# Second batch's mixing: DMA transposes on SyncE's queue in place of products with the identity

## The chip, the cores and the metric

The kernel runs on one core of one Trainium2 chip. The metric is the device time of one execution in microseconds (us). The engines are TensorE (PE; its weight loads are shown as PEld), VectorE (DVE), ScalarE (ACT), GpSimd (POOL) and SyncE (SP); SP does nothing here but issue DMAs. Each engine takes its instructions strictly in the order in which they were written.

## The reference

An attention over beacons and tokens is followed by a low-rank mixing over tokens and a two-layer perceptron, for 8 batches of 576 tokens, 8 heads of 64, 512 channels, rank 32 and 2048 hidden channels:

```
a   = softmax(mask(q @ concat(beacon_k, k)^T / 8))          # per batch and head
x   = (a @ concat(beacon_v, v)) laid out as [token, channel] # 576 x 512 per batch
h   = (x^T @ U) @ V                                          # U: 576 x 32, V: 32 x 576
u   = x + h^T
out = u + relu(u @ w_ch1) @ w_ch2
```

## The kernel before

**Layout.** Tokens of a batch lie in five tiles of 112, 128, 128, 128 and 80 rows (tile 4 is the last). The attention writes x, in 16 bits, to a tile `xb` with tokens on partitions (line 425, one DVE product per head). The perceptron wants u with channels on partitions, in one long constant tile `uT` (4 groups of 128 channels by 8 x 576 tokens). The mixing of a batch makes that change of layout and adds the low-rank part. `mix_units` gives it in two forms:

- Not turned: TensorE multiplies x with the identity into PSUM (`x_into`, line 432), 16 products for tiles 0 to 3 and four for tile 4, adds the low-rank product on top (lines 478 and 491), and the sum is copied to `uT`: two copies by DVE and two by ACT for tiles 0 to 3 (lines 467 and 469), one by DVE for tile 4.
- Turned: five DMA transposes, one per token tile, issued on SP's queue, bring x into `uT` (line 444). TensorE makes only the low-rank product, and DVE adds it to what lies in `uT`: four additions for tiles 0 to 3, one for tile 4 (line 465).

In both forms `head` comes first: 20 small products (line 453) and a DVE copy to `qts` (line 459) that make x^T U. Batch 0 is mixed by a function of its own, `first_mix`. Before the change batch 1 is mixed in the first form and batches 2 to 7 in the second.

**Perceptron.** It goes over blocks of 512 tokens. A block is 32 units of work in a queue: 16 g-units (line 559, four products of 512 columns, then a rectification by ACT or DVE) and 16 quarter-sums called c-units here (line 585, four products of 512 columns). Four quarters make one 128-row piece of the output; after its last quarter, block 0 also has four products that add u (line 593), and then DVE or ACT copies the piece (lines 602 and 600) and SP stores it (line 604). I number the c-units of block 0 by their place in the queue: c0 to c15. c0 to c3 need the first half of the second weight matrix `w2`, c4 to c7 the second half; POOL issues the two halves at line 205. The last quarters are c5, c7, c11 and c15. Block 1 needs tokens 512 to 1023, so `uT` of batch 1 must be there before its first g-unit.

**Order of the work.** The program is one hand-written order. Attention goes by pairs of heads (pair 8 is the first of batch 2). A string says what comes next: `r` regroups a pair's q and k on DVE (lines 279 and 281), `q` and `k` turn them on TensorE (line 286) and copy them from PSUM on DVE (lines 319 and 324), `v` makes scores on TensorE (line 398) with the exponentials on ACT (line 407), `m` masks on DVE (lines 335 and 337), `a` and `b` are the products with v for the two heads (lines 416, 424, 425), and `f` takes the next entry from the perceptron's queue. An entry can be empty (`None`): then an `f` does nothing. `mix(1)` places the mixing of batch 1 into the queue; after it come

```
        fill(8)
        regroup_of(NP1)
        regroup_of(NP1 + 1)
        fill(8)
        play("q8 f k8 f v8:01 f q9 f k9 f r10 v8:23,9:0 f")
```

and then the strings of `third`, the first of which is `r11 q10 f m8 k10 f v9:123 f a8 b8 q11 f`. When `mix(1)` is called, the queue holds c0 to c15.

**PSUM.** There are eight banks, handed out in turn in the order in which they were given back in the program.

**Loads.** POOL issues the loads of q, k, v and the weights (lines 199 to 228 and 674); they change the type on the way and share the 16 DMA engines with SP's queue.

Of the kernel before, what the change touches and what calls it, by code (L numbers as in the profile page):

```python
# [30 lines left out]
def kernel(  # L31
# [732 lines left out]
    NF = 2  # L764
# [24 lines left out]
    def feed(b):  # L789

        while state["t"] < NBLK and 512 * (state["t"] + 1) <= S * (b + 1):
            t = state["t"]
            units, state["part"] = mlp_units(
                512 * t, 512, lambda i, m, t=t: rows[ds(512 * t + P * i, m), :], t % 2, t > 0, t == NBLK - 1
            )
            queue.extend(units)
            state["t"] += 1

    def mix(b):

        turned = b >= NF
        turn, head, parts = mix_units(xbs[b], S * b, turned)
        if turned:
            turn()
        n = 0 if not turned else LAG + 3 if b == B - 1 else min(LAG, len(queue) - 8)
        k = 2 if turned else 1
        most, end = parts
        rest = queue[n + k + 3 :]
        queue[:] = queue[0:n] + [head] + queue[n : n + k] + [most] + queue[n + k : n + k + 3] + [end]
        for _ in range(4):  # L810
            queue.extend(rest[:1] + [None])
            del rest[:1]
        queue.extend(rest)
        feed(b)
# [23 lines left out]
    with tc.manual_schedule(engines={ENG.PE, ENG.Activation, ENG.DVE, ENG.SP, ENG.Pool}):  # L838
# [89 lines left out]
        for line in (  # L928
# [6 lines left out]
            if line.startswith("f e4"):  # L935
                load_batch(2)
        mix(1)

        fill(8)
# [81 lines left out]
        for p in range(NP1, NP):  # L1021
            b, c = divmod(p, NH2)
# [17 lines left out]
            else:  # L1040
                long_slot(p, c, av_of(p), qk or [lambda: None] * 2)
        mix(B - 1)
        guard()

# [106 lines left out]
```

## Time and profile before

| what | value |
|---|---|
| median of 3 runs | 351.85 us (351.06 to 354.78) |
| profiled execution: its time | 349.58 us |
| profiled execution: span | 347.9 us |
| PE busy | 340.4 us, 98% of the span |
| DVE busy | 190.6 us, 55% |
| ACT busy | 163.3 us, 47% |
| POOL busy | 102.9 us, 30% |

How to read it: the profiled execution's time is 1.7 us above its span, which is what lies around the span. It is 2.3 us under the median of the timed runs, so a difference is worked out within the profiled execution and then put on the median. In the rows of the timeline the columns are start in us, duration in us, engine, line, operation, output and input, shapes and count, and in brackets the idle time before it with what ended it. A matmul's end is modelled, so the start of the next group says best how long a group held the engine.

### The profile page before, as it was taken

What the parts mean: (1) busy time and instruction counts of PE and PEld (TensorE: products, weight loads), DVE (VectorE), ACT (ScalarE), POOL (GpSimd) and SP (SyncE); (2) the same over time, 40 slices, a digit from 0 to 9 for tenths busy, and PEclk for the clock granted to TensorE, in tenths of its full rate; (3) what the DMA queues carried; (4) which work ended last, traced back from release to release, by engine and by line L of the source; (5) the groups of instructions that cost most, each with busy time, mean ns of one, the idle gap of its engine ahead of it and who ended that gap; (6) DMA issues with size and microseconds to landing.
All of it is one profiled execution on the core that took longest, in us unless ns stands there. A gap on an engine that the chain in (4) does not pass through costs nothing.

```text
span 347.9 us, 7800 instructions
## 1 busy us (share of the span) xinstructions
PE 340.4 (98%) x3094; PEld 173.8 (50%) x3094; DVE 190.6 (55%) x501; ACT 163.3 (47%) x358; POOL 102.9 (30%) x147
## 2 busy tenths in 40 slices
PE   7899999999999999999999999999999999999995
PEld 3564565455554455445554554455445444444443
DVE  6686865788875653664565456535655542323311
ACT  5958851577823665077605662476344203202400
POOL 8978706754504568004820320000000000000000
PEclk9999999999999999999999999999999999999999
DMA  8999999999996999994999797613123314013011
GB/s 169 137 179 154 178 201 175 226 146 147 132 145 134 158 164 135 161 193 37 138 137 225 75 124 113 183 32 70 61 75 47 71 60 121 2 60 106 18 64 64
DMA packets 146667, 41.90 MB, mean 120 GB/s; under 512 B 131520, under 2 KB 142080, under 8 KB 146624
## 3 DMA queue, kind: packets, MB, share of 16 engines
q0 software_dynamic: 87568, 18.18, 67.8%
q1 hardware_dynamic: 58832, 22.87, 36.6%
q8 instruction: 26, 0.43, 0.5%
q10 hardware_dynamic: 224, 0.30, 0.3%
q14 instruction: 17, 0.14, 0.1%
HBM read 37.45 MB, written 9.44 MB: 135 GB/s over the span
## 4 chain that ended last, share of the span: by engine, by line
PE 84%; DMA 8%; ACT 3%; DVE 2%; POOL 1%; issue 0%; ACTq 0%; DVEq 0%
PE gps L559 35%; PE cps L585 31%; PE po L416 7%; PE sps L398 5%; DMA st<-in_q_dram 5%; ACT expt L365 2%; DMA st<-in_k_dram 2%; DMA stk<-in_k_dram 1%; PE cph L611 1%; PE tps L286 1%; ACT w L365 1%; DVE pr L279 1%; PE qtp L453 1%; PE sps L359 1%; POOL st L213 1%; PE ups L478 1%
## 5 line engine op out<-in xcount | busy, mean ns | idle before, releaser
L559 PE MATMUL gps<-uT,w 128*128 128x512 f16 x576 | 135.4, 379 | 0.5 <-DVE kT L324 0.3
L585 PE MATMUL cps<-w,gT 128*128 128x512 f16 x560 | 130.9, 379 | 0.0
L407 ACT ACTIVATE expt<-sps 128x496 f16<-128x496 f32 (+2 forms) x192 | 82.1, 540 | 75.9 <-PE sps L398 75.9
L572 ACT ACTIVATE gT<-gps 128x512 f16<-128x512 f32 x86 | 51.3, 621 | 74.6 <-PE gps L559 72.3
L559 PEld LDWEIGHTS <-w 128*128 128x128 f16 x576 | 52.1, 98 | 59.2 <-issue 2.8
L585 PEld LDWEIGHTS <-gT 128*128 128x128 f16 x560 | 50.8, 98 | 57.6 <-issue 4.6
L574 DVE TENSOR_SCALAR gT<-gps 128x512 f16<-128x512 f32 x58 | 39.9, 690 | 45.6 <-PE gps L559 44.4
L598 DVE TENSOR_TENSOR ob<-cps,ut 128x512 f32<-128x512 f32 x31 | 21.4, 691 | 49.5 <-PE cps L585 48.7
L228 POOL DMA_DIRECT2D vs<-in_v_dram x50 | 39.7, 808 | 14.9 <-DMA w<-in_moe_w_ch_dram 10.8
L416 PEld LDWEIGHTS <-expt 128*128 128x128 f16 x900 | 34.3, 97 | 12.0 <-issue 0.4
L416 PE MATMUL po<-vs,expt 128*128 128x65 f16 x900 | 36.2, 194 | 0.2
L425 DVE TENSOR_TENSOR xb<-po,rec 128x320 f16<-128x320 f32 x64 | 31.5, 492 | 2.2
L424 DVE RECIPROCAL rec<-po 128x5 f32<-128x5 f32 x64 | 12.0, 188 | 27.0 <-PE po L416 26.8
L335 DVE TENSOR_TENSOR expt<-expt,bigmask 128x512 f16<-128x512 f16 x54 | 22.5, 417 | 3.3 <-ACT expt L407 3.3
L398 PE MATMUL sps<-qT,kT 64*128 64x80 f16 (+4 forms) x288 | 22.6, 281 | 0.1
L365 ACT ACTIVATE expt<-sps 128x496 f16<-128x496 f32 (+2 forms) x48 | 20.4, 569 | 0.6 <-PE sps L359 0.6
L210 POOL DMA_DIRECT2D vs<-in_beacon_v_dram x8 | 4.3, 534 | 54.8 <-PE po L416 54.1
L674 POOL DMA_DIRECT2D st<-in_q_dram x20 | 17.0, 865 | 6.8 <-DVE xb L425 2.4
L398 PEld LDWEIGHTS <-kT 64*128 64x128 f16 x288 | 10.2, 94 | 16.0 <-issue 11.4
L674 POOL DMA_DIRECT2D st<-in_k_dram x20 | 16.9, 880 | 1.3 <-DMA st<-in_q_dram 0.9
L465 DVE TENSOR_TENSOR uT<-ups,uT 128x496 f16<-128x496 f32 x24 | 14.5, 668 | 3.7 <-PE ups L478 3.7
L319 DVE COPY qT<-tps 128x576 f16<-128x576 f16 (+1 forms) x16 | 11.8, 736 | 6.0 <-PE tps L286 3.3
(107 smaller groups left out, 179.0 us busy)
## 6 DMA issues: line engine op xcount, KB each, us to landing
out_dram<-ob SPq DMA_DIRECT2D x35, 256.0 KB, 2.2
vs<-in_v_dram POOLq DMA_DIRECT2D x18, 128.0 KB, 6.9
w<-in_moe_w_ch_dram POOLq DMA_DIRECT2D x4, 512.0 KB, 6.6
w<-in_moe_w_ch_dram POOLq DMA_DIRECT2D x2, 1024.0 KB, 12.9
st<-in_k_dram POOLq DMA_DIRECT2D x12, 128.0 KB, 9.4
st<-in_q_dram POOLq DMA_DIRECT2D x12, 128.0 KB, 10.2
st<-in_k_dram POOLq DMA_DIRECT2D x4, 288.0 KB, 12.2
st<-in_q_dram POOLq DMA_DIRECT2D x4, 288.0 KB, 13.1
```

The lines of the kernel that those rows point to most:

```text
L228: nc.gpsimd.dma_start(out=dst[a : a + nq[j], j, :, :], in_=src[hs, ds(q0[j], nq[j]), :].rearrange("h p d -> p h d"))
L335: nc.vector.tensor_tensor(out=e4, in0=e4, in1=bigmask, op=ALU.min)
L365: nc.scalar.activation(out=ex[i][:, ds(SLOT * g, gw[g])], in_=ps[g, i][:, 0 : gw[g]], func=AF.Exp, scale=scale)
L398: nc.tensor.matmul(banks[i][:, ds(at0 + o, w)], kT[hp, c, ds(P * ch, P)], qT[hp, c, ds(qa, w)], start=True, stop=True, skip_group_check=le ...
L407: nc.scalar.activation(out=at[p][3][i][:, ds(SLOT * g, gw[g])], in_=bank[:, ds(at0, gw[g])], func=AF.Exp, scale=scale)
L416: nc.tensor.matmul(po[:, j, :], ex[0 : nk[c], ds(blk[(c, j)], P)], vs[0 : nk[c], ds(c * H * E + h * E, E)], start=(c == 0), stop=(c == j),)
L425: nc.vector.tensor_tensor(out=xb[:, :, ds(h * D, D)], in0=po[:, :, 0:D], in1=r.broadcast_to([P, NT, D]), op=ALU.mult)
L559: nc.tensor.matmul(g[:, 0:n], w1[:, cc, ts(dc, P)], uT[:, cc, ds(t0, n)], start=(cc == 0), stop=(cc == NCC - 1))
L572: nc.scalar.activation(out=gT["t"][:, dc, 0:n], in_=g[:, 0:n], func=AF.Relu)
L574: nc.vector.tensor_scalar_max(out=gT["t"][:, dc, 0:n], in0=g[:, 0:n], scalar1=0.0)
L585: nc.tensor.matmul(ps[:m, :], gT["t"][:, dc, ds(P * i, m)], w2[:, dc, :], start=(dc == 0), stop=turned and dc == NDC - 1, skip_group_check ...
L674: nc.gpsimd.dma_start(out=dst[a : m[j], j, :, :], in_=src[:, ds(q0[j], nq[j]), :].rearrange("h p d -> p h d"))
```

## The change

Batch 1 is mixed in the turned form, like batches 2 to 7; `NF`, which also says where the attention's second part begins, stays 2.

```
     def mix(b):
 
-        turned = b >= NF
+        turned = b >= 1
         turn, head, parts = mix_units(xbs[b], S * b, turned)
         if turned:
             turn()
```

What `mix` does with `turned` (unchanged lines): the five transposes are issued at once, and the mixing's three units are put at another place of the queue.

```
        n = 0 if not turned else LAG + 3 if b == B - 1 else min(LAG, len(queue) - 8)
        k = 2 if turned else 1
        most, end = parts
        rest = queue[n + k + 3 :]
        queue[:] = queue[0:n] + [head] + queue[n : n + k] + [most] + queue[n + k : n + k + 3] + [end]
        for _ in range(4):
            queue.extend(rest[:1] + [None])
            del rest[:1]
        queue.extend(rest)
```

With 16 entries in the queue and `LAG` of 10, `n` becomes 8 where it was 0. The queue (a dash is an empty entry):

```
before: head c0 most c1 c2 c3 end c4 - c5 - c6 - c7 - c8 c9 c10 c11 c12 c13 c14 c15
after:  c0 c1 c2 c3 c4 c5 c6 c7 head c8 c9 most c10 c11 c12 end c13 - c14 - c15 - -
```

The functions that the turned form calls:

```
        def turn():
            for j in range(NT):
                nc.sync.dma_start_transpose(
                    out=uT[:, :, ds(u0 + q0[j], nq[j])], in_=xb[: nq[j], j, :]
                )
...
        def settle(i, dst, ups):
            if turned:
                nc.vector.tensor_tensor(out=dst, in0=ups, in1=dst, op=ALU.add)
            elif i % 2:
                nc.vector.tensor_copy(out=dst, in_=ups)
            else:
                nc.scalar.activation(out=dst, in_=ups, func=AF.Copy)
...
            for cc in range(NCC) if not turned else ():
                x_into(xb, ups[cc], cc, list(range(NT - 1)), 0, True)
```

On SP the five transposes stand ahead of the four stores of block 0, which came first there before.

More of the change, by code (lines that the diff above doesn't have):

```diff
@@ L799, in mix @@
     def mix(b):
-        turned = b >= NF
+        turned = b >= 1
         turn, head, parts = mix_units(xbs[b], S * b, turned)
```

## The prediction

> **What bounds the kernel now.** I read the busy times on the page first, then the chain that ended last, then who waits from 71 us to the end.
>
> ```profile
> PE 340.4 (98%) x3094; PEld 173.8 (50%) x3094; DVE 190.6 (55%) x501; ACT 163.3 (47%) x358; POOL 102.9 (30%) x147
> PEclk9999999999999999999999999999999999999999
> PE 84%; DMA 8%; ACT 3%; DVE 2%; POOL 1%; issue 0%; ACTq 0%; DVEq 0%
> PE gps L559 <- DVE kT L324: 0.3, 1, 0.3
> 71.00:110.00 39.00, 39.00 (x443) 21.37 (x442) 31.85 (x86) 23.00 (x52) 14.52 (x19) 1.00 1.71 140
> ```
>
> TensorE is busy for 98% of the span, at full granted clock in every slice, and 84% of the last chain is its own work. The fourth line is the whole answer on PE's products for the stretch from 71 us to the end: one wait of 0.3 us, at the start of it. The window (its length, then PE, PEld, DVE, ACT, POOL) has PE busy for all 39 us. So two things hold. TensorE time taken away is worth its full length, and a hole that opens in TensorE's stream ahead of 71 us is carried to the end, since nothing behind it has idle time in which to make it up.
>
> The stage that changes lies from 48.5 to 71 us. These are rows of its timeline; the last two, of a later pair of heads, are there for a price.
>
> ```profile
> 48.55 0.49 DVE L425 TENSOR_TENSOR xb<-po,rec 128x320 f16<-128x320 f32 x1
> 48.92 0.62 PE L453 MATMUL qtp<-xb,Usb 112*32 112x128 f16 x20
> 49.47 1.04 PE L585 MATMUL cps<-w,gT 128*128 128x512 f16 x4
> 50.34 1.05 PE L432 MATMUL ups<-ident,xb 112*128 112x112 f16 x16
> 51.32 0.39 PE L478 MATMUL ups<-Vsb,qts 32*128 32x496 f16 x4
> ...
> 54.24 0.31 PE L432 MATMUL uend<-ident,xb 80*128 80x80 f16 x4
> 54.39 0.31 PE L491 MATMUL uend<-Vend,qts 128*128 128x80 f16 x4
> ...
> 56.26 0.39 PE L593 MATMUL cps<-ident,uT 128*128 128x128 f16 x4
> 56.48 1.89 PE L585 MATMUL cps<-w,gT 128*128 128x512 f16 x8
> ...
> 59.30 0.42 PE L286 MATMUL tps<-ident,pr 96*128 96x96 f16 x6
> 59.75 0.76 DVE L319 COPY qT<-tps 128x576 f16<-128x576 f16 x1 [1.66 <-PE tps L286]
> 60.88 0.76 DVE L319 COPY kT<-tps 128x576 f16<-128x576 f16 x1 [0.37 <-PE tps L286]
> 61.77 0.58 PE L398 MATMUL sps<-qT,kT 64*128 64x496 f16 x4
> 63.58 0.69 DVE L602 COPY ob<-cps 128x512 f32<-128x512 f32 x1 [1.87 <-PE cps L593]
> 64.97 0.76 DVE L319 COPY kT<-tps 128x576 f16<-128x576 f16 x1
> 65.72 0.57 DVE L279 COPY pr<-st 96x768 f16<-96x768 f16 x1
> 68.38 0.73 DVE L319 COPY qT<-tps 128x576 f16<-128x576 f16 x1
> 70.80 1.04 PE L559 MATMUL gps<-uT,w 128*128 128x512 f16 x4 [0.33 <-DVE kT L324]
> 85.29 0.35 DVE L279 COPY pr<-st 96x768 f16<-96x768 f16 x1
> 86.17 0.76 DVE L319 COPY qT<-tps 128x576 f16<-128x576 f16 x1
> ```
>
> From start to start a c-unit holds TensorE for 50.34 - 49.47 = 0.87 us, `head` for 0.55, the four u products of a finished piece for 0.22. Note the last wait at 70.80: the second g-unit of block 1 waited for a DVE copy. From 65.72 on, DVE's row of regroupings, copies and masks is what ends there. That g-unit is my finish line: from it on both programs have the same instructions in the same order, and TensorE is gapless.
>
> **What is removed.** The 20 identity products: 51.32 - 50.34 = 0.98 us and 54.39 - 54.24 = 0.15 us, together 1.13 us of TensorE. Two copies leave ACT, which is idle there and gains nothing.
>
> **What is moved.** The queue puts c0 to c7 ahead of `head`, so pair 8 starts behind 13 c-units where it stood behind 9. From pair 8 to block 1's first g-unit only c13, c14 and c15 are left as cover, where seven were. That matters because pair 8 is a chain of hand-overs: q8 is turned on PE (59.30), copied by DVE (59.75), k8 copied (60.88), then scored on PE (61.77). In the kernel before, c-units fill these holes. In the changed one the entry behind k8 is empty, so TensorE must wait out DVE's copy, and the same DVE chain then runs on through pairs 9 and 10 to the finish line.
>
> **What is added.** Five transposes on SP, five DVE additions in place of three copies, and a wait of DVE on the transposes. Their prices:
>
> ```profile
> L465 DVE TENSOR_TENSOR uT<-ups,uT x24: 664/665/676, 105.3 to 285.5; 128x496 f16<-128x496 f32 x24
> L465 DVE TENSOR_TENSOR uT<-uend,uT x6: 479/480/481, 109.0 to 286.7; 128x320 f16<-128x320 f32 x6
> L205 POOL DMA_DIRECT2D w<-in_moe_w_ch_dram x2: 882/883/884, 36.2 to 38.6; - x2
> DMA to landing us min/median/max: 11.6/12.9/14.2
> L553 SPq DMA_TRANSPOSE ut<-uT x4: 1245/1318/2147, 69.8 to 73.8; - x4
> DMA to landing us min/median/max: 8.6/9.2/10.2
> L444 SPq DMA_TRANSPOSE uT<-xb x5: 1251/1276/2093, 92.4 to 98.5; - x5
> DMA to landing us min/median/max: 4.4/5.5/6.9
> L228 POOL DMA_DIRECT2D vs<-in_v_dram x10: 732/873/1029, 48.0 to 68.9; - x10
> DMA to landing us min/median/max: 8.0/9.2/12.4
> 50.00:55.00 5.00, 5.00 (x46) 2.79 (x45) 1.52 (x3) 1.06 (x2) 1.88 (x3) 1.00 1.32 202
> 70.00:75.00 5.00, 4.67 (x62) 2.71 (x60) 3.77 (x11) 3.42 (x8) 2.83 (x4) 1.00 2.80 164
> ```
>
> (The landing line under each row is that row's, from the windows 44 to 75 for line 228, 60 to 110 for the 553 row, 90 to 110 for the 444 row.)
>
> *When do the transposes land?* Batch 1's x is complete at 48.55 + 0.49 = 49.04. SP has nothing else, issues one about every 1.3 us, and so starts the fourth at 53.0 and the fifth at 54.3. The four additions for tiles 0 to 3 each need the first four transposes. No transpose runs in this stretch before, so I bound the flight: 4.4 us at the low end (line 444 from 92 us, where the engines have pauses), 12.4 us at the high end (a POOL load of this very stretch). The DMA columns (share, GB/s) of 50 to 55 us show 1.32 at 202 GB/s: the engines are full, as they are at 70 to 75, where line 553 took 8.6 to 10.2. I take 8.6, the nearest row's low end, since the share is lower here: the fourth lands at 61.6.
>
> [...]
>
> *The walk through the changed kernel*, by the prices above. c0 starts where `head` did, at 48.9; c3 ends at 52.4. c4 needs the second half of `w2`: issued at 38.6, landing after 14.2, so 52.8, and I take 53.0 with its hand-over, a wait of 0.6 that did not exist. c4 to c7 with two sets of u products end at 56.9, `head` at 57.5, c9 at 59.2. The low-rank products start there, and DVE, 0.45 us behind PE as at 59.30 and 59.75, could add from 59.65. It waits until 61.6. Queued behind it on DVE are the c11 copy, the last addition, and the copies of q8 and k8, for which TensorE's scores, and ACT's exponentials after them, wait. So from 61.6: four additions 2.66, line 602 0.69, last addition 0.48 make 65.4; q8's copy 0.76 and k8's 0.89 (60.88 to 61.77) make 67.05, where the scores start. TensorE has been through c12, q8, c13 and k8 by about 64.4 and stands idle some 2.6 us. Scores 0.58 and c14 0.87: 68.5. DVE takes up q9 0.45 later; q9 0.76 and k9 0.75 (64.97 to 65.72): 70.45. Then two regroupings. They took 68.38 - 65.72 = 2.66 us beside POOL's issues; one free of them took 86.17 - 85.29 = 0.88. POOL's v loads are out by 68.9 in the kernel before, so I take 2 x 0.88: 72.2. From there to the finish line as before, 70.80 - 68.38 = 2.42: **74.6 against 70.80, 3.8 us later**. The 1.13 us saved are in the walk already.
>
> Other cover: SP's first store is ready near 55.6, when the fifth transpose is just issued; even were that issue a microsecond longer, a store has four output buffers behind it. The later transposes and loads move with the rest.
>
> **Sum.** The profiled execution has 349.58 us (span 347.9 and 1.7 around it), so 353.4; on the median of 351.85, **355.7 us**, which is 1.1% slower. About 1% is what a measurement of this kernel can tell from no change. The law is simple: past 59.65, each microsecond by which the fourth transpose is later is one more at the end. With slow regroupings add 0.9.
>
> **Rivals.**
>
> *The transposes are early enough.* If they fly as from 92 us (4.4 to 6.9), the fourth lands between 57.4 and 59.9 and DVE waits for nothing worth naming. The last addition then waits for its products (about 63.15), the scores start at 65.3, and the finish line moves by 2.0 us, 2.9 with slow regroupings: 353.9 to 354.8. For it: the gentler share at 50 us. Against it: 202 GB/s there against 164 at 70 us.
>
> *They are much later.* POOL's loads are large and many here; if each transpose waits its turn behind them as those loads do behind each other, the flight is that of line 228, 12.4 us: 65.4, and the finish line moves by 7.6: 359.5. For it: the full engines. Against it: only some of the ten v loads took that long. [...]
>
> *Not slower.* The holes at 60 to 72 us are paid back behind the finish line, and 1.13 us stay as gain: 350.7. It decides from the point at which TensorE has 4.9 us of waiting behind 71 us that an earlier ACT or DMA could remove. The wait list has 0.3, so this would need the modelled ends to hide idle time.
>
> *The change does not do what it says* I exclude: the built instruction order has the 40 rows less on PE (20 products, 20 weight loads) and the five transposes on SP.
>
> **How the numbers follow.** Forecast 0.57: flight 6.9 to 10.2 us, so 2.1 to 6.3 us slower with either regrouping; 0.42 of it lies above 1% (3.5 us), 0.15 below. Early transposes 0.18, all within 1%. Much later 0.15, slower by over 1%. Not slower 0.06, within 1%. What is left, 0.04, I split: 0.02 for faster by over 1%, for which I know no mechanism, and 0.02 within. That gives slower 0.57, same 0.41, faster 0.02. The range goes from 353.0 (the early case, with a microsecond for the spread of medians) to 360.0 (just past a 12.4 us flight); outside it are the not-slower case and the worst of the late one.
>
> **What would show it.** c4 waiting for the load of `w2` until near 53 us; the first addition of line 465 waiting for a DMA at 59.6 until about 61.6; the scores of pair 8 near 67 with 2.6 us of PE idle ahead of them, named as a wait for DVE's kT copy; block 1's second g-unit near 74.6; and the same spacing as before from there to the end. Wrong would be: additions that wait for PE only, or a finish line moved by 4 us and a span that is not.

## The result and the profile after

The changed kernel takes 356.5 us (median of 6 executions, 355.2 to 357.3); the kernel before takes 351.3 us beside it (6 executions, 349.6 to 354.8). The ratio is 1.016, with a 95% interval of 1.012 to 1.019: the change makes the kernel 1.6% slower. The forecast was 355.7 us. Ratios, here and below, leave out executions more than 1.5% above the fastest of the same kernel, which are four of the kernel before and seven of e7's twelve.

The profiled execution after the change took 356.36 us (span 354.7), 6.78 us more than the profiled 349.58 of before. The medians differ by 5.2 us; the profiled execution of before was the fastest of its six. First the lines of the page that answer to those shown of before: busy times, granted clock in 40 slices, shares of the chain that ended last.

```profile
PE 342.8 (97%) x3074; PEld 174.0 (49%) x3074; DVE 190.5 (54%) x503; ACT 162.1 (46%) x356; POOL 103.1 (29%) x147
PEclk9999999789999999999999999999999999999999
PE 86%; DVE 4%; ACT 3%; DMA 3%; issue 2%; SPq 1%; ACTq 0%; DVEq 0%
```

TensorE has 20 instructions fewer and is busy 2.4 us longer. The row of the clock says how that can be: it has two slices below full, around 62 to 80 us. In the chain DVE has grown from 2 to 4%, "issue" from 0 to 2%, and 1% of SP's queue is new. The windows of the kernel after put the same in numbers (length, then busy time of PE, PEld, DVE, ACT and POOL, then granted clock, DMA share and GB/s).

```profile
48.00:71.00 23.00, 18.69 (x133) 8.63 (x130) 9.64 (x22) 2.56 (x5) 8.58 (x12) 0.90 1.52 194
71.00:75.00 4.00, 4.00 (x42) 2.44 (x41) 3.48 (x9) 1.20 (x3) 3.53 (x5) 0.71 1.50 202
75.00:110.00 35.00, 34.40 (x405) 18.86 (x404) 28.58 (x83) 24.71 (x57) 13.92 (x18) 1.00 2.16 126
```

From 48 to 71 us TensorE stands still for 4.3 us, and from 71 to 75 us it is busy at 0.71 of its clock. In windows of 0.1 us the granted clock is at half from 66.53 to 73.36 us. Behind 75 us it runs as before. The waits of TensorE in the kernel after, from 74 us to the end, are again one line:

```profile
PE gps L559 <- DVE kT L324: 0.5, 1, 0.5
```

The timeline of the kernel after, from the first c-unit to the finish line (block 1's second g-unit); a bracket is the wait ahead of an instruction and what ended it.

```profile
48.97 3.62 PE L585 MATMUL cps<-w,gT 128*128 128x512 f16 x16
49.21 7.80 SPq L444 DMA_TRANSPOSE uT<-xb  x5
53.16 1.89 PE L585 MATMUL cps<-w,gT 128*128 128x512 f16 x8 [0.57 <-DMA w<-in_moe_w_ch_dram]
57.15 0.47 PE L453 MATMUL qtp<-xb,Usb 112*32 112x128 f16 x20
59.38 0.39 PE L478 MATMUL ups<-Vsb,qts 32*128 32x496 f16 x4
...
63.24 2.42 DVE L465 TENSOR_TENSOR uT<-ups,uT 128x496 f16<-128x496 f32 x4 [3.92 <-PE tps L286]
66.58 0.74 DVE L319 COPY qT<-tps 128x576 f16<-128x576 f16 x1
68.11 0.98 PE L398 MATMUL sps<-qT,kT 64*128 64x496 f16 x4 [3.72 <-DVE kT L324]
69.03 1.89 PE L585 MATMUL cps<-w,gT 128*128 128x512 f16 x4
70.71 1.18 PE L286 MATMUL tps<-ident,pr 96*128 96x96 f16 x12
72.84 0.55 DVE L279 COPY pr<-st 96x768 f16<-96x768 f16 x1
75.16 0.74 DVE L319 COPY qT<-tps 128x576 f16<-128x576 f16 x1
77.58 1.04 PE L559 MATMUL gps<-uT,w 128*128 128x512 f16 x4 [0.49 <-DVE kT L324]
```

The products were there at 59.8, but DVE's first addition began at 63.24. The bracket names TensorE, which had long been done with the operands of that addition; what came last was the fourth transpose. The trace gives its flight. These are line 444's rows (duration of the issue in ns, first and last start, then us from issue to landing): all five, then the first and second, then the third and fourth, each from a short window around them.

```profile
L444 SPq DMA_TRANSPOSE uT<-xb x5: 1282/1327/2216, 49.2 to 55.5; - x5
DMA to landing us min/median/max: 7.6/8.9/9.9
L444 SPq DMA_TRANSPOSE uT<-xb x2: 1282/1304/1327, 49.2 to 50.6; - x2
DMA to landing us min/median/max: 7.6/8.3/8.9
L444 SPq DMA_TRANSPOSE uT<-xb x2: 1309/1762/2216, 51.9 to 53.3; - x2
DMA to landing us min/median/max: 9.8/9.9/9.9
```

One by one they were issued at 49.2, 50.6, 51.9 and 53.3 and took 7.6, 8.9, 9.9 and 9.8 us, so they landed at 56.8, 59.5, 61.8 and 63.1: the first three further apart than they were issued. Behind the additions the copies of q8 and k8 waited on DVE, and for those TensorE's scores (3.72 us). The finish line came at 77.58 instead of 70.80, which is 6.78 us later, and the profiled execution is 6.78 us longer: the whole loss lies ahead of the finish line, and nothing is paid back behind it.

### The profile page after: what moved, and what is told of

Its sections match the earlier page's. It is cut to its first block, busy times and chain, and to the rows that moved or that the text cites. A ratio compares the mean times of both kernels' runs of the same rounds, so it can differ in the third digit from the quotient of the medians.

```text
span 354.7 us, 7773 instructions
## 1 busy us (share of the span) xinstructions
PE 342.8 (97%) x3074; PEld 174.0 (49%) x3074; DVE 190.5 (54%) x503; ACT 162.1 (46%) x356; POOL 103.1 (29%) x147
## 4 chain that ended last, share of the span: by engine, by line
PE 86%; DVE 4%; ACT 3%; DMA 3%; issue 2%; SPq 1%; ACTq 0%; DVEq 0%
PE gps L559 35%; PE cps L585 31%; PE po L416 8%; PE sps L398 6%; ACT expt L365 2%; DMA uT<-xb 1%; DMA stk<-in_k_dram 1%; PE tps L286 1%; PE cph L611 1%; SPq L444 1%; PE sps L359 1%; ACT w L365 1%; DVE pr L279 1%; DVE uT L465 1%; PE qtp L453 1%
## 5 line engine op out<-in xcount | busy, mean ns | idle before, releaser
L398 PE MATMUL sps<-qT,kT 64*128 64x80 f16 (+4 forms) x288 | 23.4, 284 | 3.8 <-DVE kT L324 3.7
L465 DVE TENSOR_TENSOR uT<-ups,uT 128x496 f16<-128x496 f32 x28 | 16.9, 666 | 7.7 <-PE tps L286 3.9
L398 PEld LDWEIGHTS <-kT 64*128 64x128 f16 x288 | 10.3, 94 | 19.5 <-issue 11.6
```

Of the source, the lines that this page charges most:

```text
L398: nc.tensor.matmul(banks[i][:, ds(at0 + o, w)], kT[hp, c, ds(P * ch, P)], qT[hp, c, ds(qa, w)], start=True, stop=True, skip_group_check=le ...
```

## The experiments

The theory to be tested: the loss is the wait for late transposes in a queue order that has too little other work for TensorE at that place. Rivals: the place alone, the additions' own cost, and delayed loads. The table has one profiled execution of each kernel. "Start" is the first c-unit (or `head`, where that comes first), "finish" is block 1's second g-unit, "stage" the distance of the two, and "time" the profiled execution's time less 349.58. "Ratio" is of the timed executions, against the kernel before on the same chip.

| kernel | start | finish | stage | finish later by | time | ratio, 95% interval |
|---|---|---|---|---|---|---|
| before | 48.92 | 70.80 | 21.88 | | | |
| after | 48.97 | 77.58 | 28.61 | 6.78 | 6.78 | 1.016 [1.012, 1.019] |
| e1: place alone | 49.12 | 74.19 | 25.07 | 3.39 | 3.53 | 1.004 [1.001, 1.008] |
| e2b: no transposes | 48.94 | 71.89 | 22.95 | 1.09 | 1.17 | 1.003 [1.000, 1.006] |
| e2: transposes early | 53.28 | 77.13 | 23.85 | 6.33 | 6.07 | 1.016 [1.011, 1.020] |
| e3: hole filled | 49.99 | 76.72 | 26.73 | 5.92 | 5.73 | 1.013 [1.009, 1.018] |
| e4: two more transposes | 49.23 | 82.24 | 33.01 | 11.44 | 11.37 | 1.027 [1.022, 1.032] |
| e5: old place | 49.26 | 82.44 | 33.18 | 11.64 | 11.42 | 1.028 [1.022, 1.033] |
| e6: fewer loads | 49.33 | 80.03 | 30.70 | 9.23 | 9.63 | 1.025 [1.020, 1.030] |
| e7: more cover | 48.94 | 71.62 | 22.68 | 0.82 | 1.61 | 1.008 [1.003, 1.012] |
| e7, again | 48.91 | 71.58 | 22.67 | 0.78 | 5.66 | |
| e9: v loads first | 49.06 | 75.84 | 26.78 | 5.04 | 4.98 | 1.012 [1.007, 1.017] |
| e10: cover, v first | 49.36 | 76.18 | 26.82 | 5.38 | 5.61 | 1.011 [1.006, 1.016] |
| e11: e10, copies on ACT | 48.88 | 74.27 | 25.39 | 3.47 | 3.58 | 1.011 [1.006, 1.017] |

Except for the two rows of e7, the fifth and sixth columns agree within 0.4 us: the finish line decides.

### The new place with the old products

```
-        turned = b >= 1
+        turned, late = b >= NF, b >= 1
-        n = 0 if not turned else LAG + 3 if b == B - 1 else min(LAG, len(queue) - 8)
+        n = 0 if not late else LAG + 3 if b == B - 1 else min(LAG, len(queue) - 8)
-        k = 2 if turned else 1
+        k = 2 if late else 1
```

> Only the new place in the queue: batch 1 is mixed by products with the identity as in the kernel before, but its three units stand where the changed kernel has them (behind c7, c9 and c12). No transposes, no additions. My theory (the lost cover of pairs 8 to 10 costs about 2 to 3 us, the late transposes the rest): walking the kernel before's rows, pair 8 is turned near 63.9 us, scored near 66.2 where it was 61.8, and block 1's second g-unit stands at 73.7 to 74.6 against 70.8, so 2.9 to 3.8 us slower than before, with TensorE at full clock. Rival (the five additions on VectorE are the cost): not slower than before, within 1 us. Rival (the transposes delay the loads): not slower either.

The stage grew by 25.07 - 21.88 = 3.19 us, inside the range expected of the place. By the medians the kernel lost 2.5 us and by the ratio 1.5, so in time it is less than in this trace. In its timeline TensorE waits for `w2` at c4, and for DVE's copies at pair 8 and at the finish line, without any transpose:

```profile
53.60 1.89 PE L585 MATMUL cps<-w,gT 128*128 128x512 f16 x8 [0.86 <-DMA w<-in_moe_w_ch_dram]
...
66.61 0.58 PE L398 MATMUL sps<-qT,kT 64*128 64x496 f16 x4 [0.93 <-DVE kT L324]
...
74.19 1.04 PE L559 MATMUL gps<-uT,w 128*128 128x512 f16 x4 [0.98 <-DVE kT L324]
```

So the place costs something by itself: 3.19 us with the wait for `w2`, 2.33 without it. That is less than half of the stage's loss in the changed kernel (6.73).

### The turned form without transposes

```
+        if b > 1:
             turn()
...
-                nc.vector.tensor_tensor(out=dst, in0=ups, in1=dst, op=ALU.add)
+                nc.vector.tensor_tensor(out=dst, in0=ups, in1=other(dst), op=ALU.add)
```

For batch 1, `other` is the part of `uT` with batch 0's u.

> The changed kernel without the five transposes; the additions keep their place and size but take batch 0's u as their second operand, so x of batch 1 is left out. In the run with early transposes the stage itself, from c0 to block 1's second g-unit, was 2.0 us longer than before (23.85 against 21.88), but the transposes at 24 to 30 us held up loads on which TensorE then waited from 36 us. Without them my theory gives 2.0 to 2.9 us slower than before, first addition near 59.7 us, clock 1.00. Rival (the additions' own time): about 5 us, as the changed kernel. Rival (the transposes only delay loads): about 1 us faster than before.

Less was lost than expected: 1.07 us in the stage. The timeline shows why it is less: c0 to c5 run unbroken (24 products from 48.94), without the wait for `w2`, and pair 8's wait is short.

```profile
48.94 5.34 PE L586 MATMUL cps<-w,gT 128*128 128x512 f16 x24
...
64.39 0.58 PE L398 MATMUL sps<-qT,kT 64*128 64x496 f16 x4 [0.92 <-DVE kT L324]
...
71.89 1.04 PE L560 MATMUL gps<-uT,w 128*128 128x512 f16 x4 [1.02 <-DVE kT L324]
```

The additions and the place together cost 1.07 us here; adding the five transposes gives the changed kernel, and adds 28.61 - 22.95 = 5.66. With the 1.13 us of products that it doesn't make put back, e2b's stage grew by 2.20 us. The stage of e1, which makes these products, grew by 2.33 without its wait for `w2`. So the additions add next to nothing to the place, and additions that are dear by themselves are ruled out.

### The transposes earlier

Five transposes of the same size, of batch 0's x, stand right behind `w2` in the program, and batch 1 is mixed without transposes of its own.

```
         emit_w2()
+        mix_units(xbs[0], S, True)[0]()
...
+        if b > 1:
             turn()
```

> The changed kernel with transposes that cannot be late: they read batch 0's x (complete near 36 us) and are issued there, so batch 1's u is made from batch 0's x, and everything else stays, the additions and their place too. My theory: the additions wait for TensorE only and start near 59.7 us, the hole ahead of pair 8's scores is about 1 us instead of 3.7, the clock stays at 1.00, and the kernel is 2.0 to 2.9 us slower than before (the changed one: 5.2). Rival (the additions' own time): as slow as the changed kernel, about 5 us. Rival (the transposes delay the loads of 50 to 60 us): the 1.1 us of saved products show, about 1 us faster than before.

The expectation missed the total. The stage was indeed short (23.85), but it started 4.3 us later: SP issued the transposes from 23.7 to 30.1 us, not near 36, and there they fell among loads on the path. Where the kernel before had no such wait, TensorE waited 0.79 us for v and 1.19 for weights of the first layer, as this row of its timeline shows. Behind that four products of 512 columns held it for 1.72 us, where they hold it for 0.87 elsewhere, and its clock was at 0.91 over the window from 30 to 48 us.

```profile
39.23 1.79 PE L559 MATMUL gps<-uT,w 128*128 128x512 f16 x4 [1.19 <-DMA w<-in_moe_w_ch_dram]
```

Earlier transposes are no way out here, since something on the path pays for them there.

### The hole filled with products

The string of pairs 8 to 10 is cut behind k8, and 16 products with the identity, which nobody reads, are put into the hole.

```
-        play("q8 f k8 f v8:01 f q9 f k9 f r10 v8:23,9:0 f")
+        play("q8 f k8 f")
+        idle(16, ident)
+        play("v8:01 f q9 f k9 f r10 v8:23,9:0 f")
```

> The changed kernel with 16 products of the identity with itself (about 3.5 us, results unused) in TensorE's hole between k8 and the scores of pair 8. The hole and VectorE's wait stay as long. If the clock of 0.71 from 71 to 75 us follows from the hole, the clock stays at 1.00, c14 takes 0.87 us instead of 1.68, and the kernel is 1 to 2.5 us faster than the changed one, so 3 to 4.5 us slower than before. If the low clock has another cause, or costs nothing since VectorE ends last there, it is as slow as the changed kernel: 5 to 6 us slower than before.

The scores follow the products of the hole without a wait; c14 behind them takes 69.71 - 68.84 = 0.87 us, where it took 70.71 - 69.03 = 1.68 in the changed kernel. Its timeline, and the clock, which in the changed kernel was at half over the same products (0.55 in this window):

```profile
63.45 2.42 DVE L465 TENSOR_TENSOR uT<-ups,uT 128x496 f16<-128x496 f32 x4 [5.13 <-PE tps L286]
...
68.33 0.58 PE L398 MATMUL sps<-qT,kT 64*128 64x496 f16 x4
68.84 1.04 PE L585 MATMUL cps<-w,gT 128*128 128x512 f16 x4
69.71 0.69 PE L286 MATMUL tps<-ident,pr 96*128 96x96 f16 x12
```

```profile
66.00:71.00 5.00, 5.00 (x36) 2.31 (x34) 3.10 (x7) 1.96 (x4) 1.88 (x3) 1.00 1.69 197
```

So in the changed kernel the clock fell because of the hole. The stage is 1.88 us shorter than in the changed kernel, but 0.81 of it comes ahead of the additions (63.45 - 49.99 = 13.46 us from the start, where it was 63.24 - 48.97 = 14.27). Behind the scores it is 8.39 us instead of 9.47 to the finish line, so the clock's share is about 1.1. In time, each against the kernel before beside it, the gain is 0.2 us by the medians (5.0 against 5.2) and 0.8 by the ratios (4.7 against 5.5), and the intervals of the two ratios overlap: that the hole brings the half clock is shown by the trace, its worth in time isn't settled.

### Two more transposes ahead of the five

```
+        for j in (1, 2) if b == 1 else ():
+            nc.sync.dma_start_transpose(
+                out=uT[:, :, ds(2 * S + q0[j], nq[j])], in_=xbs[b][: nq[j], j, :]
+            )
         if turned:
             turn()
```

> The changed kernel with two more transposes of batch 1's x ahead of the five on SyncE's queue; they write tokens of batch 2 that are written again later, so nothing is left out. My theory's law (each microsecond by which the fourth transpose is later is one more at the end): it is issued about 2.6 us later and lands 2.6 to 3.3 us later, the additions start near 66 us, and the kernel is 7.5 to 9 us slower than before. If the additions or the place in the queue set the time, it is as slow as the changed kernel, about 5.

The kernel got 10.2 us slower by the medians and 9.4 by the ratio, a little more than expected. In its timeline the first addition is now named as waiting for the transposes. It begins 4.59 us later than in the changed kernel, and the finish line comes 4.66 later: one for one.

```profile
67.83 2.42 DVE L465 TENSOR_TENSOR uT<-ups,uT 128x496 f16<-128x496 f32 x4 [9.90 <-DMA uT<-xb]
...
72.70 0.98 PE L398 MATMUL sps<-qT,kT 64*128 64x496 f16 x4 [3.49 <-DVE kT L324]
```

### The turned form at the old place

```
-        turned = b >= 1
+        turned, late = b >= 1, b >= NF
```

with `n` and `k` by `late`, as in the first experiment.

> Transposes and additions as in the changed kernel, but batch 1's three units at their old place in the queue (ahead of c0, c1 and c4). The transposes still land near 63.2 us, the additions still wait for them, and behind them on VectorE now stand the c5 copy and the regroupings of pairs 8 and 9 too: scores of pair 8 near 70.7 us, TensorE idle for some 8 us and at a low clock after it: 9 to 11 us slower than before, 4 to 6 slower than the changed kernel. If the place in the queue is what costs (rival), this is the faster one: at most 2 us slower than before.

The kernel lost 10.0 us by the medians. DVE's additions stand ahead of the regroupings there, so TensorE waits 9 us for `pr`:

```profile
64.85 2.42 DVE L465 TENSOR_TENSOR uT<-ups,uT 128x496 f16<-128x496 f32 x4 [14.60 <-DMA uT<-xb]
...
68.67 0.66 PE L286 MATMUL tps<-ident,pr 96*128 96x96 f16 x6 [9.02 <-DVE pr L279]
```

With transposes this late the new place is the better one of the two, so the place isn't the main cost of the change.

### Without batch 2's v loads

```
-            emit_loads(b, Ls[b], vss[b % 2])
+            emit_loads(b, Ls[b], vss[b % 2], b != 2)
...
+        if with_v:
             v_loads(v[b], beacon_v[b], vs)
```

Batch 2 computes with batch 0's v.

> The changed kernel without the loads of batch 2's v, which POOL issues from 48 to 58 us beside the transposes (batch 2 then works with batch 0's v, which is what is left out). If queued loads make the transposes late, their flight falls from 8.9 us at the median to 5 to 7, the first addition starts at 60 to 62 us where it was 63.24, the hole falls under 3 us, and the kernel is 1.5 to 4 us faster than the changed one, so 1 to 3.5 slower than before. If a transpose takes that long by itself, nothing changes: 5 us slower than before.

This went the wrong way: 8.8 us slower than before by the medians, where the changed kernel lost 5.2. The transposes flew longer, and the first addition began 3.04 us later. This kernel's transposes, then a row of its timeline (lines are numbered one higher):

```profile
L445 SPq DMA_TRANSPOSE uT<-xb x5: 1245/1327/1949, 49.6 to 55.6; - x5
DMA to landing us min/median/max: 7.6/10.2/12.5
```

```profile
66.28 2.42 DVE L466 TENSOR_TENSOR uT<-ups,uT 128x496 f16<-128x496 f32 x4 [7.58 <-issue]
```

With the v loads gone, POOL issued batch 3's k and q loads in their place, while the transposes flew. What these do differently is seen in the DMA queues: pieces recorded, MB, share of 16 engines (q0 has POOL's loads, q1 has SP's transfers). The kernel after, from 54 to 58 us and from 60 to 62 us:

```profile
q0 software_dynamic: 779, 0.57, 91.5%
q1 hardware_dynamic: 778, 0.19, 36.6%
...
q1 hardware_dynamic: 738, 0.17, 84.1%
q0 software_dynamic: 739, 0.11, 80.3%
```

and the kernel of this experiment, from 60 to 62 us:

```profile
q0 software_dynamic: 396, 0.29, 91.8%
q1 hardware_dynamic: 400, 0.09, 37.2%
```

In each of these windows the queues move nearly one piece for one. The loads' pieces have some 0.57 MB / 779 = 730 bytes where k and q are loaded, and 0.11 MB / 739 = 150 where v is; the transposes' have about 240 in both. Beside the first kind the transposes get 0.19 MB in 4 us, so one of 128 KB takes 2.8 us; beside the second 0.17 MB in 2 us, so 1.5. SP issues one every 1.3 us. The landings of the changed kernel, 2.7, 2.3 and 1.3 us apart, fit this. So by these counts it isn't how many loads are queued that spreads the landings, but how large the pieces are that move beside theirs, and this experiment put larger ones there (0.29 MB / 396 = 730 bytes from 60 to 62 us). In which order the pieces of the two queues go, the counts don't show. They also leave out the start of a flight: in the changed kernel q1 moves no piece before 53.2 us, 4.0 us after the first issue, while q0 moves 0.80 MB from 49 to 53 us, at 200 GB/s. What the transposes wait for until then isn't shown.

### The v loads ahead of the second half of k and q

In `emit_loads`, for batch 2 alone, `v_loads` moves ahead of the second half of the k and q loads.

```
+            if v_first and hs is HALVES[1]:
+                v_loads(v[b], beacon_v[b], vs)
```

> The changed kernel with batch 2's v loads (pieces of 128 bytes) moved ahead of the second half of its k and q loads (768 bytes) on POOL's queue; nothing is left out. In the traces a transpose's piece and a load's piece go one for one: 778 and 779 between 54 and 58 us, when the loads' pieces are large, 738 and 739 between 60 and 62, when they are small, so 2.66 us a transpose against 1.39. By that the first addition starts at 60 to 61 us where it was 63.24, the clock stays near 1.00 and the kernel is 2 to 3.5 us slower than before (the changed one 5.2). If the amount queued ahead is what counts, nothing changes: 5 us.

This tests the size of the pieces, with small ones beside the transposes and no load left out. The flights fell to between 7.6 and 8.1 us, and the first addition came 1.7 us earlier than in the changed kernel. From 56 to 60 us q1 moved 1506 pieces and 0.37 MB, q0 1720 and 0.23 MB: q0's pieces have some 134 bytes, and a transpose of 128 KB takes an estimated 1.4 us, but the counts differ, so one for one isn't a law. The rows of its timeline, then its window from 66 to 71 us (lines are numbered three higher):

```profile
61.53 2.42 DVE L468 TENSOR_TENSOR uT<-ups,uT 128x496 f16<-128x496 f32 x4 [2.73 <-issue]
...
66.40 0.98 PE L401 MATMUL sps<-qT,kT 64*128 64x496 f16 x4 [2.29 <-DVE kT L327]
```

```profile
66.00:71.00 5.00, 4.60 (x28) 2.19 (x28) 1.62 (x4) 1.96 (x4) 2.92 (x4) 0.66 1.33 218
```

The direction is as expected, the additions half a microsecond later than that. The hole is smaller, but the clock fell to half all the same, for about 3.4 us (0.66 over these 5). The finish line gained 1.74 us (75.84 against 77.58), and the kernel is 1.2% slower than before, 5.1 us by the medians and 4.2 by the ratio, which is more than expected.

### More cover, and other orders

The queue of e7 puts `head` behind c7 and the two sets of low-rank products behind c13 and c14, with empty entries between, so that pair 8 and most of pair 9 go ahead of the additions:

```
+        c = queue[:]
...
+        if b == 1:
+            queue[:] = c[0:8] + [head, c[8]] + [None] * 6 + c[9:13]
+            queue.extend([both(c[13], most), both(c[14], end), c[15]])
```

> Transposes and additions as in the changed kernel, but the c-units that cover pairs 8 to 10 stay where they were in the kernel before: c0 to c7, head, c8, then one c-unit at each place from q8 to q10, the four additions behind the k9 copy and the last behind regrouping 10. The transposes land before the additions are reached; what remains is 3.1 us more for VectorE in the row that ends last at block 1's second g-unit, less 1.13 us of TensorE: 1.1 to 2.0 us slower than before, 3 to 4 faster than the changed kernel. If the lost cover does not matter, it is as slow as the changed one: 5 us.

The stage lost only 0.80 us, less than expected. The additions no longer wait for transposes, as the first row of its timeline shows. Yet its twelve executions spread from 350.3 to 358.6 us, and their median, 356.0, is 5.2 above the kernel before: over all of them the cover gained nothing.

```profile
64.51 2.42 DVE L465 TENSOR_TENSOR uT<-ups,uT 128x496 f16<-128x496 f32 x4 [0.35 <-PE ups L478]
```

A second profile was to show where the rest comes from.

> A second look at the kernel that keeps the cover: its profiled execution was 0.8 us behind the kernel before at block 1's second g-unit, yet its timed runs went from 350.3 to 358.6 us. If the transposes sometimes land after the additions are reached, a slow execution shows the first addition later than 64.5 us with TensorE idle behind it and a clock under 1.00. If it is something else, a slow execution shows the same stage and is longer elsewhere.

It took 355.24 us with the same stage (22.67). The loss lies far behind: in batch 3's mixing the additions waited for their transposes, TensorE waited 1.9 us in all for the additions, and its clock was at 0.89 from 150 to 165 us. Rows of its timeline and of its windows:

```profile
148.51 2.41 DVE L465 TENSOR_TENSOR uT<-ups,uT 128x496 f16<-128x496 f32 x4 [6.44 <-DMA uT<-xb]
149.24 0.34 PE L398 MATMUL sps<-qT,kT 64*128 64x208 f16 x3 [1.25 <-DVE uT L465]
```

```profile
150.00:165.00 15.00, 14.33 (x99) 6.38 (x98) 7.36 (x20) 8.35 (x18) 0.00 (x0) 0.89 1.27 168
```

In the profiles of before and after, line 465 waits for TensorE alone behind 74 us (3.7 us in both). In e7's first profile the additions of batch 3 waited for transposes too, but 3.9 us where it is 6.44 here, and TensorE lost 0.2 us by it. So in e7 later transposes are late as well, more in one execution than in another. That a shifted stream of loads makes them so is likely and not tested, and of e7's longer executions only this one was profiled. Whether the executions of the kernel before that took 353 to 356 us are such ones isn't known: none of them was profiled.

The last two kernels join what had worked. e10 is e7 with the v loads first; in e11 ACT takes over the two large copies of pair 9:

```
-        copies = [(act_copy, nc.vector.tensor_copy) if p == 0 else (nc.vector.tensor_copy,)] * 2
+        copies = [(act_copy, nc.vector.tensor_copy) if p == 0 else (act_copy if p == 9 else nc.vector.tensor_copy,)] * 2
```

> The kernel that keeps the cover (additions behind the k9 copy), with batch 2's v loads ahead of the second half of its k and q. The transposes land near 60 to 61 us, well ahead of the additions at 64.5, so the spread of 350 to 358 us should shrink: 1 to 2 us slower than before. Against it: k and q of pairs 10 and 11 land near 66 to 67 us, where they are wanted at 67; if they are late, VectorE waits for them at the regroupings and the kernel is 2 to 4 us slower than before.

> As the one before, with the two large copies of pair 9 on ACT, which idles there, in place of VectorE: 1.5 us less on the engine that ends last at block 1's second g-unit. 0 to 1 us slower than before, 0.5 to 1.5 faster than the one before; equal to that one if VectorE does not end last.

The spread is small in e10's six executions (354.2 to 355.6 us), but the q and k of pair 10, which now load later, are late, and TensorE waits for them. From e10's timeline:

```profile
70.92 0.35 DVE L282 COPY pr<-st 96x768 f16<-96x768 f16 x1 [1.58 <-DMA st<-in_q_dram]
...
71.34 0.54 PE L289 MATMUL tps<-ident,pr 96*128 96x96 f16 x6 [1.99 <-DVE pr L282]
```

e11 waits for the same loads (1.86 us at TensorE) and stayed 1.1% slower than before (353.2 to 356.3 us), where at most 1 us had been expected. No order tried here is faster than the kernel before.

## Why the prediction was right

**What bounds the kernel**: right. In twelve of the thirteen changed executions in the table (counting after), the loss at the finish line is the loss at the end within 0.8 us; only e7's second execution lost more behind it.

**What is removed, and the wait for `w2`**: right. c4 waited 0.57 us (forecast 0.6) and ran at 53.16 (53.0); the low-rank products came at 59.38 (59.2). The 1.13 us of TensorE are saved, and are all that the change could have gained. The second half of `w2` was issued at 38.6 us here as in the forecast. The wait for it isn't the same in every execution: 0.86 us in e1, none in e2b.

**When the transposes land**: right in kind, short by 1.64 us. The first addition was forecast for 61.6 and came at 63.24. The fourth transpose was issued at 53.3, not 53.0, and flew 9.8 us, not 8.6, which had been the low end of line 553's flights. The median of the five was 8.9.

**Additions to scores**: 63.24 to 68.11 is 4.87 us where 5.45 were worked out, as the four additions and the copies overlap a little (2.42 us for the four together, and 1.53 from q8's copy to the scores). The hole of TensorE, forecast as 2.6 us, was 3.72 and named as foretold, a wait for DVE's kT copy.

**Scores to the next regrouping**: the step that was missed. Forecast 3.40 us, measured 72.84 - 68.11 = 4.73, so 1.33 more. The sum put the hole's effect on the clock at nothing and priced scores and c14 at full clock; they ran at half of it. e3 shows the cause: with the hole filled, the clock stays at 1.00 and c14 takes 0.87 us. In windows of 0.1 us the changed kernel is at half clock for 6.83 us, from 66.53 to 73.36. For the others the mean clock of their windows gives the length, taken as time at full and at half clock, as an estimate: 3.4 us in e9 (0.66 over 5 us) and e10 (0.57 over 4), 3.3 in e7's second profile (0.89 over 15), 3.2 in e2 (0.91 over 18), 6.8 in e6, 10.3 in e4 and e5, so in all of them near one, two or three times 3.4. The fall came at 66.53 us, 2.1 us after the last product ahead of the hole (64.39), and in e9 after a hole of 2.29 us. What sets the moment of the fall isn't shown.

**The regroupings**: 2.32 us, forecast 1.76, so 0.56 more, part of the 0.9 set aside for slow ones: POOL, which the forecast had done by 68.9, was still issuing then (3.53 us of 4 busy from 71 to 75 us). That its issuing slows DVE's copies is the forecast's reading; no run tests it. From there to the finish line it was 2.42 us, as forecast.

So the terms were off by +1.64, -0.58, +1.33 and +0.56, together 2.95 us, and 3.8 us in the profiled execution became 6.8. On the medians 3.8 became 5.2, and 356.5 us lies 0.8 above the forecast. That it is so close is partly luck: the forecast started from a median of 351.85, 0.5 above the 351.3 measured beside the change, and the profiled execution of before was the fastest of its six.

**The rivals**. Early transposes are refuted, as they flew 7.6 to 9.9 us. Much later ones (12.4 us) didn't come, though e6 shows that they can (12.5). The reason given for that rival, a transpose that waits behind POOL's loads, isn't settled: no piece of q1 moved before 53.2 us, but from 54 us on the two queues moved nearly one piece for one (778 and 779 from 54 to 58 us, 519 and 510 from 58 to 60, 738 and 739 from 60 to 62). The not-slower rival is refuted by the finish line, which moved as much as the end.

**The parts of the loss**. In stages of one profiled execution each: place and additions without transposes 1.07 us (2.20 less the 1.13 saved), the kernel with transposes 5.66 more; of these 0.57 is c4's wait for `w2`, which e1 has without transposes, and about 1.1 are the clock, by e3. The law of the prediction, each microsecond of the fourth transpose one at the end, held where the transposes were late already: in e4 (4.59 us later, 4.66 at the finish line) and e9 (1.71 earlier, 1.74), less well in e6 (3.04 later, 2.45). From transposes that cost no wait it doesn't hold: e2b's first addition began at 59.04, so 4.20 us earlier than in the changed kernel, and its finish line came 5.69 earlier. There the half clock comes on top.

**What stays open**: why e1 lost 3.5 us in its profile and 1.5 by its ratio (its wait for `w2`, 0.86 us, is one part that another execution may not have), what the transposes wait for in their first 4 us, and how often later batches' transposes are late in kernels that are not e7.

## What to carry to other kernels

Before work is moved from a full TensorE to a transfer, look at what its consumer's engine has queued behind the wait, and at what the DMA queues carry at that moment: here 1.13 us of products were exchanged for a flight of 9.8. Where the transposes got about one piece for each piece of the loads (778 and 779 from 54 to 58 us), their pace went with the size of the loads' pieces, an estimated 2.8 us for 128 KB beside 730 bytes and 1.5 beside 150, and not with the number of loads (none was left out in e9, where the flights fell to between 7.6 and 8.1 us). A hole in TensorE's stream should be priced with the slower clock that can follow it: behind 3.72 us of idling here it cost about 1.1 us more, by e3.

## What the runs showed of the hardware that was not expected

- SP's queue, with the transposes, and POOL's loads moved nearly equal numbers of pieces in the changed kernel (778 and 779 from 54 to 58 us, 738 and 739 from 60 to 62 us), less equal ones in e9 (1506 and 1720 from 56 to 60). By the bytes in these two windows of the changed kernel a transpose of 128 KB takes an estimated 2.8 us beside pieces of 730 bytes and 1.5 beside pieces of 150; taking small-piece loads away made the first addition 3.04 us later (e6).
- A hole of 2.29 us in TensorE's work was followed by about 3.4 us at half clock (e9; 0.66 over the window from 66 to 71 us), and so was one of 1.99 us (e10: c-unit of 1.71 us behind it, 0.57 from 71 to 75 us). One of 1.86 us left the clock at 1.00 (e11: c-unit of 0.86), as did the waits of 0.92 and 1.02 us in e2b. In e7's second profile five waits within 3.6 us, the longest of 1.25, were followed by half clock too (0.89 from 150 to 165 us), so it isn't the longest hole alone that decides.
- Transposes issued 25 us earlier, far from their consumer, cost as much as late ones (6.33 against 6.78 us at the finish line). TensorE waited 1.98 us for loads there, and its clock was at 0.91 from 30 to 48 us.
